# First rows of an attention and dense-layer kernel: where keys, values and M land in the on-chip memory

## The chip, the cores and the metric

The program runs on one core of a Trainium2 chip. A core has TensorE (PE in the profile, with its weight loads as PEld), VectorE (DVE), ScalarE (ACT), GpSimd (POOL) and SyncE (SP), which issues nearly all DMAs here, and 16 DMA engines. The metric is the device time of one execution in microseconds (us), the median of the runs.

## What is computed

For B = 4 batches, H = 8 heads, S = 576 rows and D = 64, causal softmax attention is mixed with a read from a memory M, and the result goes through a dense layer of 512 to 2048 to 512 with a leaky nonlinearity per column:

```python
scores = scale * np.matmul(q, k.transpose(0, 1, 3, 2))      # causal mask, softmax -> a
local = np.matmul(a, v)
mem_out = einsum('bhsd,bhde->bhse', phi(q), M_prev) / (einsum('bhsd,bhd->bhs', phi(q), z_prev)[..., None] + 1e-06)
x = g * mem_out + (1 - g) * local                            # g: sigmoid(beta) by head
h = x @ w_in
out = (np.maximum(h, 0.0) + alpha * np.minimum(h, 0.0)) @ w_out
```

## The kernel before, in words

The 576 rows of a batch are cut into a first block of 64 rows and four blocks of 128. The first 64 rows of all four batches are a case of their own, called Z in the code: two tiles t of two batches each. Their work opens the program; the blocks of the batches follow, and with each group of 256 rows goes its part of the dense layer (moe_in, in the trace matmuls named h; moe_out, named y).

The opening, in order: load_first issues the loads (phases LZ for q, Lz for z_prev, LK for k, LV for v and M). first_scores(t) transposes q and k of tile t on PE (phase tZ; ACT copies the results back), makes the 64 x 64 score products of two batches and eight heads (phase sZ), and DVE reduces each with its mask while ACT takes the exponentials. They land in columns 64 to 127 of each head in the buffer P. prep_vZ (phase v4) finds the largest sums of squares of v and of M over all batches: ACT squares the two value tiles, DVE takes their maximum, PE turns it, DVE reduces it, and scales come of it. prep_phi (phases p40, p41, p4) makes phi(q), its norm, and puts the scaled phi(q) into columns 0 to 63 of P. first_values(t) (phase oZ) scales the probabilities in P, transposes P on PE into a PT buffer, and multiplies that by the tile of 128 partitions that holds M in its lower and v in its upper half, so that one product gives memory part and local part together. Its output is x for the first matmuls of the dense layer in float32 (phases h4_100 to h4_103), which read the first half of w_in (loads LW00 to LW03, conversions C00 to C03 on DVE, from 64-bit floats). 40 matmuls on a tile of ones without any use of their result (phases N and n) stand between the first ones on PE.

In the opening k of Z lies in R[14], the two tiles of M and v in R[15] and R[16]; R holds weights later. q and z lie in buffers with the tag q2. PT is a ring of four buffers of 128 x 1152 words, of which the opening uses two in first_values.

The order is written out by hand: PLACES gives each operation of each phase its place in one list for all engines, and issue sends them out in that list's order. Each engine, and each DMA queue, works through its own in that order. cells and price belong to the tool that found the places: cells tells which parts of a buffer an operation touches, price holds its estimates; they change nothing in the program once PLACES is there.

Of the kernel before, what the change touches and what calls it, by code (L numbers as in the profile page):

```python
# [33 lines left out]
        "38 55"  # L34
    ),
    "LZ1": (
        "39 37"
    ),
    "Lz": (
        "16 17 0"  # L40
    ),
    "LK0": (
        "78 36"
    ),
    "LK1": (
        "75 128"
    ),
    "LV0": (
        "154 79"
    ),  # L50
    "LV1": (
        "194 184"
    ),
    "I": (
        "1 10 2 7 8 9 11"
    ),
    "z": (
        "40 43 56 41 109"
    ),
    "N": (  # L60
        "6 13 14 18 19 20 21 22 23 24 25 27 28 45 46 47"
    ),
    "n": (
        "49 50 51 66 81 82 83 95 96 97 98 101 103 104 105 107 108 115 116 117 118 119 152 153"
    ),
    "J": (
        "30 31 33 42 177 26 32 34 35 48 61 63 67 74 88 90 172 102"
    ),
    "a4": (
        "68 54 87 91"  # L70
    ),
    "K": (
        "5 29"
    ),
    "tZ0": (
        "57 58 59 60 65 110 111 112 113 114 122"
    ),
    "sZ0": (
        "120 121 123 124 125 126 127 129 130 131 132 133 135 136 139 140 146 142 147 143 148 144 141 145 183 182 187 "
        "188 186 202 179 181"  # L80
    ),
    "tZ1": (
        "84 85 86 92 94 134 149 150 151 157 156"
    ),
    "sZ1": (
        "158 159 160 161 162 163 164 165 166 167 168 169 170 171 173 174 204 198 197 214 200 191 208 196 229 199 213 "
        "215 201 233 231 232"
    ),
    "v4": (
        "155 195 205 209 210 216 217 218 460 219"  # L90
    ),
    "p40": (
        "62 64 69 70 175"
    ),
    "p41": (
        "76 77 93 137 138"
    ),
    "p4": (
        "176 178 185 211 220 221 223 180 222 224 251"
    ),  # L100
    "oZ0": (
        "230 235 237 240 241 242 243 244 245 246 247 248 249 262 263 264 265 266 278 279 280 281 282 284 285 295 302 "
        "303 306 307"
    ),
    "oZ1": (
        "234 236 250 252 253 254 255 256 257 258 259 260 261 291 292 293 294 296 297 304 308 309 310 311 312 313 314 "
        "315 316 317"
    ),
    "LW00": (
        "12"  # L110
    ),
    "LW01": (
        "71"
    ),
    "LW02": (
        "80"
    ),
    "LW03": (
        "189"
    ),  # L120
    "LX00": (
        "270"
    ),
    "LX01": (
        "300"
    ),
    "LX02": (
        "238"
    ),
    "LX03": (  # L130
        "276"
    ),
    "C00": (
        "44 52 53"
    ),
    "n0": (
        "203 206"
    ),
    "C01": (
        "72 73 89"  # L140
    ),
    "n1": (
        "207 212"
    ),
    "C02": (
        "99 100 106"
    ),
    "n2": (
        "225 226"
    ),  # L150
    "C03": (
        "190 192 193"
    ),
    "n3": (
        "227 228"
    ),
    "D00": (
        "271 273 283"
    ),
    "c0": (  # L160
        "371 398 399 407 421 459 481 482 623"
    ),
    "D01": (
        "301 345 372"
    ),
    "D02": (
        "269 274 289"
    ),
    "D03": (
        "277 287 290"  # L170
    ),
    "LW10": (
        "401 400"
    ),
    "LW11": (
        "404 444"
    ),
    "C10": (
        "402 403 433"
    ),  # L180
    "c1": (
        "434 449 471 463 478 486 508 557 577 730 646 709"
    ),
    "LW12": (
        "465 466"
    ),
    "C11": (
        "445 447 448"
    ),
    "LW13": (  # L190
        "457 456"
    ),
    "C12": (
        "467 469 470"
    ),
    "C13": (
        "458 461 462"
    ),
    "L0q": (
        "338 239 267"  # L200
    ),
    "L0k": (
        "335 337 336 15"
    ),
    "L0v": (
        "473 474 475 487"
    ),
    "a0": (
        "268 272 275 388"
    ),  # L210
    "bk00": (
        "321 322 323 324 325 318 319 320 326 347"
    ),
    "bk01": (
        "346 351 352 362 348 350 358 370 363 364 366 382 375 376 377 378"
    ),
    "v0": (
        "488 492 493 489 496 497 498 502 503 505 1236 510"
    ),
    "p00": (  # L220
        "305 330 331 385 390"
    ),
    "p01": (
        "349 356 357 387 389"
    ),
    "p0": (
        "425 429 435 468 512 514 515 504 516"
    ),
    "L0Q": (
        "298 286"  # L230
    ),
    "L0K": (
        "405 339"
    ),
    "L0V": (
        "523 522"
    ),
    "A0": (
        "299 288 446 541"
    ),  # L240
    "BK00": (
        "383 384 386 410 411 393 394 395 396 409"
    ),
    "BK01": (
        "438 441 442 443 451 424 427 428 431 432"
    ),
    "V0": (
        "524 537 556 566 591 598 599 684 626 622 629"
    ),
    "r02": (  # L250
        "391 500 501 564 587"
    ),
    "r03": (
        "406 408 495 569 603"
    ),
    "r0": (
        "655 658 682 685 695 698 703 699 708"
    ),
    "h4_100": (
        "327 328 329 332 333 334 340 341 353 354 355"  # L260
    ),
    "s011": (
        "397 476 472 477 485 490 513 517 509 506"
    ),
    "P010": (
        "518 525 526 527 528 531 548 549 550 551 552 559 560"
    ),
    "h4_101": (
        "342 343 344 359 361 365 367 368 374 412 392"
    ),  # L270
    "y4_100": (
        "452 439 453 440"
    ),
    "P011": (
        "519 539 535 543 547 540 570 571 572 574 575 581 582"
    ),
    "s013": (
        "521 532 533 534 554 561 538 555 542 562"
    ),
    "P012": (  # L280
        "565 567 536 568 553 586 590 593 594 595 600 610 611"
    ),
    "o011": (
        "607 608 609 620"
    ),
    "P013": (
        "583 584 613 585 612 601 614 615 616 617 627 628 632"
    ),
    "h4_102": (
        "360 373 379 380 381 415 416 418 419 479 491"  # L290
    ),
    "y4_101": (
        "454 450 455 494"
    ),
    "s015": (
        "563 576 578 588 596 605 580 597 589 606"
    ),
    "P014": (
        "621 624 633 625 592 630 634 635 636 637 661 662 665"
    ),  # L300
    "o013": (
        "666 667 679 680"
    ),
    "P015": (
        "649 657 663 668 631 664 669 670 671 676 677 691 692"
    ),
    "s017": (
        "619 652 650 654 674 672 653 675 651 673"
    ),
    "P016": (  # L310
        "694 696 618 697 573 705 716 717 718 719 720 724 725"
    ),
    "h4_103": (
        "413 414 417 420 422 423 436 437 464 511 507"
    ),
    "y4_102": (
        "480 520 499 558"
    ),
    "o015": (
        "711 713 714 715"  # L320
    ),
    "P017": (
        "683 693 638 712 639 721 726 727 728 729 735 736 740"
    ),
    "s031": (
        "752 753 769 771 772 773 784 783 811 770 796 799"
    ),
    "P030": (
        "812 817 883 816 884 937 820 832 1029"
    ),  # L330
    "o017": (
        "747 748 749 750"
    ),
    "bv00": (
        "797 1032 745 746"
    ),
    "bv01": (
        "765 1031 794 795"
    ),
    "bv02": (  # L340
        "825 1139 733 734"
    ),
    "bv03": (
        "798 808 756 809"
    ),
    "P031": (
        "800 824 801 859 828 866 861 898 969"
    ),
    "h0_100": (
        "688 690 723 759 760 761 762 764 766 775 778"  # L350
    ),
    "y4_103": (
        "529 579 530 602 430 737 739 426 604 704"
    ),
    "h0_101": (
        "689 722 732 763 767 768 780 781 802 804 803"
    ),
    "y0_100": (
        "776 792 847 829"
    ),  # L360
    "h0_102": (
        "779 787 788 789 790 791 793 821 822 833 850"
    ),
    "y0_101": (
        "848 869 849 870"
    ),
    "h0_103": (
        "814 815 818 819 834 835 838 841 842 871 875"
    ),
    "y0_102": (  # L370
        "863 872 864 874"
    ),
    "s033": (
        "856 857 858 946 947 950 997 991 992 862 948 998"
    ),
    "P032": (
        "1087 1092 1097 1093 1131 1151 1094 1103 1241"
    ),
    "y0_103": (
        "880 885 881 886 738 882 1175 656 887 971"  # L380
    ),
    "x4": (
        "369 678"
    ),
    "x0": (
        "751 774"
    ),
    "LW20": (
        "643 640"
    ),  # L390
    "LW21": (
        "645 642"
    ),
    "C20": (
        "644 648 659"
    ),
    "c2": (
        "686 741 757 805 807 810 831 836 1091"
    ),
    "LW22": (  # L400
        "687 660"
    ),
    "C21": (
        "647 700 701"
    ),
    "LW23": (
        "742 702"
    ),
    "C22": (
        "743 744 754"  # L410
    ),
    "LW30": (
        "758 755"
    ),
    "C23": (
        "777 782 785"
    ),
    "S20": (
        "837 845"
    ),  # L420
    "S21": (
        "852 853"
    ),
    "S22": (
        "854 867"
    ),
    "S23": (
        "868 903"
    ),
    "LW31": (  # L430
        "806 786"
    ),
    "C30": (
        "813 830 839"
    ),
    "c3": (
        "843 860 928 1005 1006 1030 1090 1099 1100 1165 1102 1135 1224 1174 1303 1226"
    ),
    "LW32": (
        "846 840"  # L440
    ),
    "C31": (
        "844 851 855"
    ),
    "LW33": (
        "943 944"
    ),
    "C32": (
        "878 902 926 879 901 925"
    ),  # L450
    "C33": (
        "945 966 1000"
    ),
    "S30": (
        "1118 1133"
    ),
    "S31": (
        "1160 1162"
    ),
    "S32": (  # L460
        "1176 1177"
    ),
    "S33": (
        "1220 1222"
    ),
    "S00": (
        "1329 1330"
    ),
    "S01": (
        "1380 1548"  # L470
    ),
    "S02": (
        "1565 1588"
    ),
    "S03": (
        "1591 1673"
# [2343 lines left out]
```

## Time and profile before

| | us |
|---|---|
| median of 3 runs | 548.23 (547.07 to 548.61) |
| profiled execution | 547.6 |
| its span, first to last instruction | 545.8 |
| PE busy | 527.6 (97%) |
| DVE busy | 445.4 (82%) |
| ACT busy | 389.2 (71%) |
| POOL busy | 66.2 (12%) |

The mean granted clock of PE is 0.990. A busy share is an average over the whole span; the rows further down take it apart by stretch of time. Nearly all instructions carry the line of one helper, L1740, so they are told apart by the names of the buffers that they write and read: R is the weights' buffer and also that of k, v and M of the first rows, y, h, s and bank are accumulators, P holds probabilities, PT their transposes.

### The profile page before, as it was taken

The page shows a single profiled execution, that of the slowest core. Times are in us where ns is not written, and L with a number is a line of the kernel's source. Part 1 is how long each engine was busy: PE and PEld are TensorE (multiplying, and loading weights), DVE is VectorE, ACT ScalarE, POOL GpSimd, SP SyncE. Part 2 cuts the span into 40 slices and gives each one's busy share as a digit, 9 for nine tenths or more (in the row PEclk, how much of TensorE's full clock was granted, in tenths as well). Part 3 has the DMA queues.
Part 4 walks back from the last instruction along what each step waited for, and adds up shares of the span by engine and source line. Part 5 has one row for each costly group of instructions (what it writes and reads, how often), then busy time and mean ns, then how long its engine had stood idle before and what let it go on. Part 6 is the DMA issues. An engine that isn't in the chain of part 4 may idle for free. (4 is left out here: it accounts for less than half of the span.)

```text
span 545.8 us, 11936 instructions
## 1 busy us (share of the span) xinstructions
PE 527.6 (97%) x4415; PEld 355.1 (65%) x4415; DVE 445.4 (82%) x1195; ACT 389.2 (71%) x815; POOL 66.2 (12%) x142
## 2 busy tenths in 40 slices
PE   8889999999988999999999999999999999999997
PEld 3578446748556677677756766767686667666863
DVE  3899999999999999999977999998757786662421
ACT  3678899778978689988876988777556767642322
POOL 3000040201011012111111121311102101100000
PEclk8899999999998999999999999999999999999999
DMA  8999915679578979558999765659235556270101
GB/s 166 213 243 364 234 64 182 201 231 223 129 146 181 196 182 218 134 127 166 223 206 185 179 121 99 145 135 190 65 89 119 100 118 142 75 150 11 39 1 38
DMA packets 225650, 82.33 MB, mean 151 GB/s; under 512 B 216100, under 2 KB 216116, under 8 KB 225592
## 3 DMA queue, kind: packets, MB, share of 16 engines
q1 hardware_dynamic: 225408, 81.55, 66.4%
q8 instruction: 34, 0.56, 0.4%
q14 instruction: 24, 0.20, 0.1%
q10 hardware_dynamic: 184, 0.02, 0.0%
HBM read 35.15 MB, written 5.77 MB: 75 GB/s over the span
## 5 line engine op out<-in xcount | busy, mean ns | idle before, releaser
L1740 PE MATMUL y<-R,gg 128*128 128x512 f16 (+1 forms) x832 | 230.6, 396 | 0.4 <-DVE t L1740 0.3
L1740 PE MATMUL h<-x,R 128*128 128x256 f16 x1536 | 212.8, 274 | 1.2 <-DMA x<-xn 1.2
L1740 PEld LDWEIGHTS <-R 128*128 128x128 f16 x1536 | 144.5, 98 | 36.7 <-issue 4.1
L1740 PEld LDWEIGHTS <-gg 128*128 128x128 f16 x768 | 72.7, 98 | 62.4 <-DVE gg L1740 1.0
L1740 POOL TENSOR_SCALAR E<-q,nrm,sm 128x64 f32<-128x64 f32 x112 | 54.7, 501 | 350.4 <-DVE sm L1740 272.9
L1740 ACT ACTIVATE E<-E,mx 128x320 f32<-128x320 f32 (+3 forms) x136 | 80.8, 599 | 22.6 <-DVE mx L1740 20.9
L1740 PE MATMUL bank<-v,PT 128*128 128x64 f16 x1224 | 86.2, 194 | 3.3 <-DVE xn L1740 1.8
L1740 DVE SCALAR_TENSOR_TENSOR P<-E,mx,P 128x640 f16<-128x640 f32 (+3 forms) x112 | 76.2, 699 | 12.2 <-ACT P L1740 11.7
L1740 ACT ACTIVATE P<-E,mx 128x640 f16<-128x640 f32 (+3 forms) x112 | 72.0, 674 | 19.9 <-POOL E L1740 11.4
L1740 PEld LDWEIGHTS <-PT 128*128 128x128 f16 x1224 | 67.1, 98 | 21.8 <-issue 2.7
L1740 DVE SCALAR_TENSOR_TENSOR r<-r,oma,h 128x256 f32<-128x256 f32 x128 | 57.3, 473 | 24.8 <-ACT r L1740 24.5
L1740 DVE CUSTOM_DVE_ANT_0 E<-s,mask,pm 128x576 f32<-128x576 f32 (+3 forms) x96 | 57.8, 613 | 7.6 <-PE s L1740 3.9
L1740 ACT ACTIVATE r<-h 128x512 f32<-128x512 f32 x72 | 42.0, 587 | 27.8 <-PE h L1740 23.5
L1740 ACT ACTIVATE gg<-r,gsc 128x512 f16<-128x512 f32 x56 | 39.5, 714 | 30.6 <-PE y L1740 23.3
L1740 DVE SCALAR_TENSOR_TENSOR gg<-r,gsc,gg 128x512 f16<-128x512 f32 x56 | 41.7, 745 | 20.1 <-ACT gg L1740 18.7
L1740 PE MATMUL s<-k,qT 128*128 128x320 f16 (+5 forms) x136 | 36.6, 290 | 0.2 <-DVE mx L1740 0.2
L1740 PE MATMUL h<-R 128*128 128x256 f32 x144 | 35.6, 391 | 0.0
L1740 PE MATMUL s<-k,qS 128*128 128x192 f16 (+4 forms) x120 | 32.6, 294 | 1.1 <-DMA qS<-qT 1.1
L1740 PEld LDWEIGHTS h<-R 128*128 128x128 f32 x144 | 26.7, 194 | 4.9 <-issue 1.5
L1740 ACT ACTIVATION_READ_ACCUMULATOR E<-E,mx 128x1 f32 x124 | 23.4, 189 | 0.0
L1740 ACT ACTIVATE xn<-bank,xsc 128x256 f16<-128x256 f32 x28 | 13.0, 466 | 10.5 <-PE bank L1740 10.1
L1740 ACT ACTIVATE t<-y,u 128x512 f32<-128x512 f32 x18 | 12.2, 678 | 11.6 <-PE y L1740 9.0
(179 smaller groups left out, 618.8 us busy)
## 6 DMA issues: line engine op xcount, KB each, us to landing
q<-in_q_dram SPq DMA_DIRECT2D x16, 256.0 KB, 4.9
vn<-in_v_dram SPq DMA_DIRECT2D x16, 256.0 KB, 4.4
out_dram<-t SPq DMA_DIRECT2D x16, 256.0 KB, 2.4
kn<-in_moe_w_in_dram SPq DMA_DIRECT2D x6, 512.0 KB, 7.9
kn<-in_moe_w_out_dram SPq DMA_DIRECT2D x6, 512.0 KB, 4.6
kn<-in_k_dram SPq DMA_DIRECT2D x12, 256.0 KB, 4.4
qS<-qT SPq DMA_DIRECT2D x24, 128.0 KB, 2.7
R<-in_moe_w_in_dram SPq DMA_DIRECT2D x4, 512.0 KB, 5.4
```

Of the source, the lines that this page charges most:

```text
L1740: fn(*a, **kw)
```

## The change

In load_first k, v and M of the first rows get three buffers of the ring PT. A transfer takes two batches at once, for q and k as it was for v and M already: q into 64 neighbouring partitions, k into every second partition of 128, v into the odd and M into the even partitions of a tile. A tile's two batches are thereby other ones: tile t now holds batches t and t + 2, and new_group writes their output rows so. The phases LZ0, LZ1, LK0 and LK1 have one DMA each in place of two.

What reads these buffers follows: first_scores takes k at every second column, the score and phi(q) columns of P are interleaved (even columns phi(q), odd columns probabilities), first_values takes v by batch pair and position, prep_vZ reduces even and odd partitions, and z is spread by two copies on ACT in place of one. cells and price learn the new shapes. All places are given anew: 6239 before, 6242 after.

```diff
@@ load_first
-        kz, v0, v1 = (R[i].rearrange("p (t h d) -> p t h d", t=2, h=H) for i in (14, 15, 16))
+        kz, v0, v1 = (wkp.tile([128, 2, H, D], F32, tag="PT", bufs=TB) for _ in range(3))
...
-        for b in range(B):
-            t, ps = b // 2, slice(b % 2 * 64, b % 2 * 64 + 64)
-            work.phase = f"LZ{t}"
-            Y.dma_start(out=qz[ps, t], in_=q[b, :, 0:64, :].rearrange("h p d -> p h d"))
+        for c in range(2):
+            work.phase = f"LZ{c}"
+            Y.dma_start(out=qz[64 * c:64 * c + 64].rearrange("p t h d -> p (t h) d"),
+                        in_=q[2 * c:2 * c + 2, :, 0:64, :].rearrange("b h p d -> p (b h) d"))
...
-        for b in range(B):
-            t, ps = b // 2, slice(b % 2 * 64, b % 2 * 64 + 64)
-            work.phase = f"LK{t}"
-            Y.dma_start(out=nat[Z]["k"][t][ps], in_=k[b, :, 0:64, :].rearrange("h p d -> p h d"))
+        for c in range(2):
+            work.phase = f"LK{c}"
+            Y.dma_start(out=kz[c::2].rearrange("p t h d -> p (t h) d"),
+                        in_=k[2 * c:2 * c + 2, :, 0:64, :].rearrange("b h p d -> p (b h) d"))
...
-            for ps, src in ((slice(64, 128), v[2 * t:2 * t + 2, :, 0:64, :]), (slice(0, 64), M_prev[2 * t:2 * t + 2])):
+            for ps, src in ((slice(1, None, 2), v[2 * t:2 * t + 2, :, 0:64, :]), (slice(0, None, 2), M_prev[2 * t:2 * t + 2])):
@@ prep_vZ
-        V.tensor_reduce(mw, pt.rearrange("p (t c) -> p t c", t=2), axis=AX.X, op=ALU.max)
+        V.tensor_reduce(mw, pt.rearrange("p (c t) -> p t c", t=2), axis=AX.X, op=ALU.max)
@@ prep_phi
-            o = p["P"][i][:, :, 0:D]
+            o = p["P"][i][:, :, 0::2]
@@ first_scores
-            for c in (slice(0, 64), slice(64, 128)):
-                T.matmul(s[c, h, :], lhsT=qT[:, h // 2, c], rhs=kT[:, h % 2, h // 2, c], start=True, stop=True)
+            for c in range(2):
+                cs = slice(64 * c, 64 * c + 64)
+                T.matmul(s[cs, h, :], lhsT=qT[:, h // 2, cs], rhs=kT[:, h % 2, h // 2, c::2], start=True, stop=True)
...
-        E = p["P"][t][:, :, 64:128]
+        E = p["P"][t][:, :, 1::2]
@@ first_values
-        E = P[:, :, 64:128]
+        E = P[:, :, 1::2]
...
-                T.matmul(o[ps, a, c], lhsT=n["v"][t][:, b, h, :], rhs=PT[:, h, c], start=True, stop=True)
+                T.matmul(o[ps, a, c], lhsT=n["v"][b][:, t, h, :], rhs=PT[:, h, c], start=True, stop=True)
@@ new_group
-            [(64 * a, 64 * a + 64, (2 * t + a) * S) for a in range(2)] for t in range(2)]
+            [(64 * a, 64 * a + 64, (t + 2 * a) * S) for a in range(2)] for t in range(2)]
@@ the spread of z
-    A.copy(zs.rearrange("p (b n) -> p b n", b=B), ident[0:B, 0:B][:, :, None].to_broadcast([B, B, 64]))
+    for t in range(2):
+        A.copy(zs[:, 128 * t:128 * t + 128].rearrange("p (b n) -> p b n", b=2),
+               ident[0:B, t:B:2][:, :, None].to_broadcast([B, 2, 64]))
```

The order of SP's loads in the opening, by PLACES, before: LW00, LK0 (second batch), LZ1 (second), LZ0, LZ1, LZ0 (second), LW01, LK1, LK0, M of LV0, LW02, LK1 (second), v of LV0, M of LV1, LW03, v of LV1. After: LW00, LZ1, LZ0, LK0, LW01, LK1, LW02, v and M of LV0, LW03, M and v of LV1. Three small loads (beta, z_prev, alpha) go out on ACT's queue at the very start in both. On PE 15 of the fillers n stand between the transposes of the second tile's k and its scores in the new order (2 in the old one), and on DVE the conversion C00 comes first, and the maximum of batch 0's first q before the scaling of the probabilities.

## Rows read from the trace of the kernel before

**Rows 1.** The page: busy time and share by engine; DVE's tenths in 40 slices.

```profile
PE 527.6 (97%) x4415; PEld 355.1 (65%) x4415; DVE 445.4 (82%) x1195; ACT 389.2 (71%) x815; POOL 66.2 (12%) x142
...
DVE  3899999999999999999977999998757786662421
```

**Rows 2.** Busy time by stretch, columns as headed.

```profile
core 0: us, PE busy (x) PEld busy (x) DVE busy (x) ACT busy (x) POOL busy (x), PEclk, DMA share, GB/s
...
6.79:31.44 24.65, 21.45 (x136) 12.89 (x136) 19.16 (x87) 14.75 (x49) 0.00 (x0) 0.86 1.07 207
36.00:75.00 39.00, 39.00 (x202) 25.42 (x200) 36.98 (x103) 32.47 (x75) 4.16 (x10) 1.00 0.91 259
75.00:140.00 65.00, 63.36 (x400) 42.48 (x399) 63.72 (x153) 55.82 (x115) 8.38 (x16) 1.00 0.64 179
140.00:200.00 60.00, 55.35 (x475) 35.88 (x474) 59.41 (x144) 48.54 (x87) 5.62 (x12) 0.97 0.82 173
200.00:260.00 60.00, 60.00 (x537) 41.65 (x535) 59.11 (x167) 53.07 (x111) 8.52 (x20) 1.00 0.75 164
260.00:540.00 280.00, 277.89 (x2602) 191.49 (x2601) 202.21 (x533) 178.95 (x374) 35.20 (x72) 1.00 0.56 116
```

**Rows 3.** The same table for five short stretches of the opening.

```profile
4.00:6.00 2.00, 1.92 (x5) 0.46 (x3) 0.00 (x0) 0.00 (x0) 1.23 (x2) 1.00 1.27 198
6.00:8.00 2.00, 1.14 (x4) 0.54 (x5) 1.03 (x7) 0.50 (x2) 0.00 (x0) 1.00 0.43 81
16.50:19.50 3.00, 2.98 (x36) 1.87 (x34) 1.44 (x5) 1.16 (x2) 0.00 (x0) 1.00 1.40 148
32.20:33.80 1.60, 1.28 (x10) 1.07 (x11) 1.60 (x3) 0.85 (x2) 0.00 (x0) 1.00 1.29 289
42.00:45.00 3.00, 3.00 (x19) 2.65 (x18) 2.80 (x6) 2.27 (x5) 0.00 (x0) 1.00 1.03 396
```

**Rows 4.** SP's issues (start, duration), and its wait for beta.

```profile
0.73 0.39 SPq L1740 DMA_DIRECT2D R<-in_moe_w_in_dram  x1
...
1.99 5.16 SPq L1740 DMA_DIRECT2D q<-in_q_dram  x4
...
18.63 0.60 SPq L1740 DMA_DIRECT2D R<-in_v_dram  x1
...
SPq L1740 <- DMA gco<-in_beta_dram: 2.6, 1, 2.6
```

**Rows 5.** Timeline: start, duration, engine, operation, count, idle time before, releaser.

```profile
26.75 1.06 ACT L1740 ACTIVATE R<-R 128x1024 f32<-128x1024 f32 x1 [1.18 <-DMA R<-in_v_dram]
...
27.93 0.16 DVE L1740 TENSOR_TENSOR stv<-stv 128x1 f32<-128x1 f32 x1 [0.20 <-ACT R L1740]
...
31.44 1.29 DVE L1740 TENSOR_TENSOR P<-P,zsm 128x512 f32<-128x512 f32 x2
...
32.28 1.07 PE L1740 MATMUL y<-ident,P 128*128 128x128 f32 x8 [1.19 <-DVE P L1740]
...
34.67 2.37 PE L1740 MATMUL s<-PT,R 128*64 128x64 f32 x64
...
37.89 2.34 PE L1740 MATMUL h<-R 128*128 128x256 f32 x10
```

**Rows 6.** Groups of 0 to 36 us: busy us, mean ns, idle before.

```profile
L1740 PE MATMUL h<-ones 128*128 128x512 f16 x40 | 13.7, 484 | 1.0 <-DVE ones L1740 1.0
...
L1740 DVE TENSOR_REDUCE stq<-q 128x1 f32<-128x512 f32 x4 | 2.7, 677 | 0.0
...
L1740 DVE CUSTOM_DVE_ANT_0 P<-s,mz 128x64 f32<-128x64 f32 x16 | 2.7, 218 | 0.0
...
L1740 DVE TENSOR_TENSOR P<-q,nrm 128x512 f32<-128x512 f32 x2 | 1.4, 686 | 0.0
...
L1740 DVE TENSOR_TENSOR P<-P,zsm 128x512 f32<-128x512 f32 x2 | 1.3, 689 | 0.0
...
L1740 DVE TENSOR_SCALAR R<-R 128x512 int32<-128x512 int32 x3 | 1.3, 424 | 0.0
```

More of the change, by code (lines that the diff above doesn't have):

```diff
@@ L33 @@
     "LZ0": (
-        "38 55"
+        "43"
     ),
     "LZ1": (
-        "39 37"
+        "42"
     ),
     "Lz": (
-        "16 17 0"
+        "7 36 0"
     ),
     "LK0": (
-        "78 36"
+        "45"
     ),
     "LK1": (
-        "75 128"
+        "51"
     ),
     "LV0": (
-        "154 79"
+        "60 64"
     ),
     "LV1": (
-        "194 184"
+        "176 175"
     ),
     "I": (
-        "1 10 2 7 8 9 11"
+        "1 23 2 24 25 26 120"
     ),
     "z": (
-        "40 43 56 41 109"
+        "30 29 49 54 31 82"
@@ L120 @@
     ),
     "LX00": (
-        "270"
+        "226"
     ),
     "LX01": (
-        "300"
+        "283"
     ),
     "LX02": (
-        "238"
+        "228"
     ),
     "LX03": (
-        "276"
+        "306"
     ),
     "C00": (
-        "44 52 53"
+        "33 34 35"
     ),
     "n0": (
-        "203 206"
+        "192 209"
     ),
     "C01": (
-        "72 73 89"
+        "74 97 108"
     ),
     "n1": (
-        "207 212"
+        "210 211"
     ),
     "C02": (
-        "99 100 106"
+        "143 155 183"
@@ L399 @@
     ),
     "LW22": (
-        "687 660"
+        "683 653"
     ),
     "C21": (
-        "647 700 701"
+        "626 692 698"
     ),
     "LW23": (
-        "742 702"
+        "741 705"
     ),
     "C22": (
-        "743 744 754"
+        "742 743 744"
     ),
     "LW30": (
-        "758 755"
+        "755 745"
     ),
     "C23": (
-        "777 782 785"
+        "772 786 789"
     ),
     "S20": (
-        "837 845"
+        "822 838"
     ),
     "S21": (
-        "852 853"
+        "839 843"
@@ L1606, in cells @@
         w = 1 if ap.dtype == F16 else 2
+        n = 1
+        for x in ap.tensor.shape[1:]:
+            n *= x
+        n = n * (1 if ap.tensor.dtype == F16 else 2) // w
+        sides = 0, 1
+        if ps == 2 * n:
+            sides = divmod(ap.offset, n)[0] % 2,
+            ps, pn = n, 2 * pn - 1
         p0, o = divmod(ap.offset, ps)
@@ L1616, in cells @@
         m, size = self.known[key], ps * w
-        return sum(m << size * h for h in range(2) if p0 < 64 * (h + 1) and p0 + pn > 64 * h), size
+        return sum(m << size * (2 * h + e) for h in range(2) if p0 < 64 * (h + 1) and p0 + pn > 64 * h for e in sides), size
     def add(self, kind, engine, name, a, kw):
@@ L1692, in price @@
                 return 630, 983, 2186, 343
+            if kb > 200 and (o.tensor.name.startswith("PT") or ins[0].tensor.name.startswith("in_q")):
+                return 640, 1250 if ins[0].tensor.name.startswith("in_q") else 950, 2200, 290
             return (700, 1736, 2490, 290) if kb > 200 else (690, 643, 2157, 150)
```

1008 lines of the change are left out of this document (504 added, 504 removed), and 96 rows, old and new, of tables.

## The prediction

> **What bounds the kernel now.** I read the busy times first, then a table by stretch, then the DMA rates of the first 45 us, then the waits in order of time up to the first dense matmul. TensorE (PE) is busy 97% of the span, VectorE (DVE) 82% [rows 1]; as averages these hide two regimes. In the table by stretch [rows 2] the reader should compare each engine's busy time with the length of its stretch. From 36 to 75 us PE is busy 39.00 of 39 us and DVE 36.98; from 75 to 260 us DVE is busy 182.24 of 185 us (63.72, 59.41 and 59.11) while PE idles 6.29 us in all (1.64 and 4.65, none after 200); from 260 to 540 us PE is busy 277.89 of 280. So from 36 us on the work is packed on PE, on DVE or on both, with 8.4 us of PE idle time in 504 us. In contrast, from 6.79 to 31.44 us DVE is busy only 19.16 of 24.65 us, and much of PE's 21.45 us is no useful work: 40 filler matmuls on a tile of ones take 13.7 us [rows 6]. The slack is in the first 32 us.
>
> What ends last there is a landing. SP issues the last v transfer at 18.63 us [rows 4]; ACT's second square of values starts at 26.75 us, ended by that DMA [rows 5]; from it the chain runs over the DVE maximum (27.93), the scales, DVE's multiplication of the probabilities (31.44) and PE's transposes (32.28, after 1.19 us of idle time for DVE) to the value products (34.67) and the first dense layer (37.89). The DMA engines explain the landing [rows 3]: with only such first-row transfers under way (256-byte runs to 64 neighbouring partitions) they are fully occupied, share 1.40, and move 148 GB/s; with the same runs to 128 partitions, share 1.29, 289 GB/s; with weights, 396 GB/s. And from 6 to 8 us they run dry (share 0.43, 81 GB/s), because the fourth q issue waits 2.6 us on SP for beta [rows 4]; behind it stand all of SP's loads.
>
> **The change, part by part.**
>
> *Landing places.* k, v and M go to every second partition of 128, q stays on 64 neighbouring ones. Bytes up to the last v: four weight halves of 512 KiB, 2.10 MB, and 2.10 MB of q, k, v and M. Before: 2.10/0.396 = 5.3 us and 2.10/0.148 = 14.2 us, together 19.5. The trace took from the first issue at 0.73 to 26.75, 26.0 us, of which I give 2.0 us to the way of the first bytes and 1.2 us to the hole at 6 to 8 us (2 us x (1 - 81/198), by the 198 GB/s of 4 to 6 us [rows 3]); the remaining 22.8 us are 1.17 times the sum, and I keep that factor. After: weights 5.3, q 0.52/0.148 = 3.5, the rest 1.57 MB. No row shows a transfer to every second partition. Its ends are 148 GB/s (no gain, 10.6 us) and 289 GB/s (as with 128 partitions, 5.4 us); a rate below 148 I exclude, since runs and bytes are the same. I take 289: the two rows differ only in the partitions reached, and every second one reaches over all 128. Sum 14.2 us, times 1.17 is 16.6, plus 2.7: the last v at 19.3 us, 7.4 us earlier. At 148 GB/s: 19.5 x 1.17 + 2.7 = 25.5, 1.2 us earlier.
>
> [...]
>
> *Pairs in one transfer.* q and k take 4 issues instead of 8 (v and M had pairs already). SP's issue time is on no path here, but the wait for beta is met at the ninth DMA of the program: before with 1 MiB issued ahead of it, after with 1.75 MiB (a weight, two of q, one of k, a weight), which at the rates above last until about 2.7 + 1.3 + 3.5 + 0.9 + 1.3 = 9.7 us, past the end of the wait at 6.5 us (1.99, three issues of 0.65, then 2.6). The hole closes; its 1.2 us are in the sum.
>
> *Buffers of their own.* kz, v and M move from R[14] to R[16] into three of the four PT buffers. The next writers there are the second first_values transpose (over kz, which has been read long before) and the first units of batch 0, later still; nothing waits, cost 0. first_values(0) now reads both value tiles; it already depended on both through the common maximum, so no wait is new.
>
> *Interleaved operands.* P is written at every second word, and k is read so by the 64 score matmuls. DVE's part is 16 score reductions of 218 ns and two products each of 686 and 689 ns, 6.2 us [rows 6]. The nearest row is the weight conversion that reads every second word: 424 ns for 512 elements, less than the 686 of a dense two-input product, so a stride of two costs a read nothing; no row shows a strided write. Bounds 0 and twice the time (+6.2 us); below 0 nothing, since elements stay the same. I take 0. ACT gets one more small copy for z, at a time when it is busy 0.50 us of 2 [rows 3]; cost 0.
>
> *New order.* All queues are permuted, few operations by much. In front it puts the maximum of batch 0's first q (677 ns [rows 6]) ahead of the product of probabilities and the first weight conversion ahead of beta's arithmetic.
>
> *What is late next.* By the landing alone, PE's transposes would start 5.5 us (32.28 - 26.75) after 19.3, at 24.8 us. But DVE has 19.16 + 0.68 = 19.84 us of work after 6.79, so its last product cannot start before 26.6 us, against 31.44: 4.8 us is the ceiling, and DVE is late next. I leave it 0.8 us of waits, chiefly for the second tile's scores, which stand behind 15 fillers on PE. Gain at the transposes: **4.0 us**. It carries through, because q, k and W_out of the next stage follow on the same queue, earlier too, and from 36 us on DVE and PE are packed. Profiled execution 547.6 (span 545.8 and 1.8 around it) - 4.0 = 543.6; the median of the runs is 0.6 above that execution, so 548.2 - 4.0 = **544.2 us**.
>
> **Rivals.**
> 1. *The landing gets no faster*: every second partition at 148 GB/s. The last v lands 1.2 us earlier: 547.0. For it: the row is missing. Against: the factor of 1.95 between rows with equal runs. Chance 0.12.
> 2. *The gain reaches the transposes and is given back between 75 and 260 us*, where the order is new and DVE is full: PE idle time there grows from 6.3 to some 9.5 us. 547.5. For it: a wait that a new order moves costs directly there; against: the amount of DVE work is unchanged. Chance 0.13.
> 3. *Slower*: in the same stretch the new order starves PE (of transposed probabilities, or of values behind DVE) for more than 4.0 + 1.6 = 5.6 us beyond the 6.3 of before, so that idle time nearly doubles; at 6.5 us more, 550.7. The clock is part of that price: idle PE time goes with granted clock 0.97 in 140 to 200 us. For it: 4.65 us of idle time sit there already. Against: DVE is full there in any order. (Strided DVE writes at twice the time, +6.2 us, would come out near 550 too; I count them here.) Chance 0.08.
> 4. *More*: the front gains its whole 4.8 us and the new order also removes half of the 4.65 us at 140 to 200 us: 541.1. Chance 0.12.
>
> **How the numbers follow.** Forecast, a gain of 2.5 to 4.8 us, 543.4 to 545.7: 0.55. A change of 0.3% (1.6 us) is about what a measurement of this kernel can tell from none. Faster by more: the forecast, rival 4 and half of rival 1 (where the landing is better than its bound): 0.55 + 0.12 + 0.06 = 0.73. Same: half of rival 1 and rival 2: 0.19. Slower: 0.08. The range 541.2 to 548.0 leaves out rival 3, half of rival 4 and the upper part of rival 2, under 0.2.
>
> **What would show it.** After the change, ACT's second square should start at 19 to 21 us; a stretch with only v and M on the queue should move well over 200 GB/s; the DMA share at 6 to 8 us should be near 1; DVE's idle time between its first work and the product of probabilities should fall from 5.5 to about 1 us; PE's transposes of P should start near 28.3 us and the first dense run near 34. The table by stretch, moved by 4 us, should show the same PE idle time (8.4 us) as before. The prediction is wrong if the landing comes early and PE's transposes do not (then DVE, ACT or a filler holds them), or if they come early and the idle time after 36 us grows.

## The result: 0.84% faster, and the profile after

| us | before | after |
|---|---|---|
| median | 548.93 (547.07 to 551.05) | 544.38 (542.94 to 545.80) |
| profiled execution | 547.6 | 544.01 |
| its span | 545.8 | 542.2 |
| mean granted clock of PE | 0.990 | 0.999 |

The ratio of the times is 0.9916, with a 95% interval of 0.9888 to 0.9944: a gain of 4.5 us, and in the profiled execution of 3.6 us (that of the kernel before, with 547.6 us, lies 1.3 us under its median). The forecast was 544.2 us. The granted clock is higher after the change, but it does not make the gain: of the runs with a mean granted clock of 0.997 or more, the 15 of the changed kernel (here, in e0 and in e10) have a median of 544.9 us and the 6 of the kernel before one of 549.7. The list of places holds 6242 operations before the change and 6239 after it: four DMAs fewer, one copy more.

The page of the changed kernel, busy times and DVE's tenths in 40 slices (for [rows 1]); the line of the helper is now L1750:

```profile
PE 523.0 (96%) x4415; PEld 352.9 (65%) x4415; DVE 444.0 (82%) x1195; ACT 391.4 (72%) x816; POOL 67.8 (13%) x142
...
DVE  4999898999999999999988899988777876752222
```

The second digit of DVE, the slice from 13.6 to 27.1 us, is now a 9, that is 90% or more. The table by stretch (for [rows 2]) has the columns us, PE, PEld, DVE, ACT and POOL busy (instructions), granted clock, DMA share, GB/s:

```profile
6.79:31.44 24.65, 22.44 (x207) 14.61 (x208) 23.45 (x97) 17.84 (x55) 0.00 (x0) 1.00 1.07 266
36.00:75.00 39.00, 38.39 (x181) 23.66 (x180) 36.32 (x111) 33.52 (x81) 7.87 (x16) 1.00 0.74 229
75.00:140.00 65.00, 63.52 (x389) 41.10 (x389) 63.26 (x143) 54.62 (x106) 6.95 (x9) 1.00 0.69 187
140.00:200.00 60.00, 52.23 (x474) 35.34 (x475) 58.93 (x145) 49.13 (x87) 6.18 (x12) 1.00 0.84 177
200.00:260.00 60.00, 59.93 (x548) 41.52 (x546) 58.37 (x162) 52.03 (x110) 9.22 (x20) 1.00 0.76 164
260.00:540.00 280.00, 276.16 (x2581) 190.65 (x2578) 198.66 (x528) 177.93 (x371) 33.29 (x72) 1.00 0.57 114
```

In the opening (first line) DVE idles 1.20 us in place of 5.49, and the DMA engines move 266 GB/s in place of 207. In the fourth line PE idles 7.77 us in place of 4.65. The timeline of the opening (for [rows 5]; start, duration, engine, operation, count, idle time before and what ended it):

```profile
20.37 1.06 ACT L1750 ACTIVATE R<-PT 128x1024 f32<-128x1024 f32 x1
21.60 0.22 DVE L1750 CUSTOM_DVE_ANT_0 P<-s,mz 128x64 f32<-128x64 f32 x1 [0.29 <-PE s L1750]
...
22.03 0.16 DVE L1750 TENSOR_TENSOR stv<-stv 128x1 f32<-128x1 f32 x1
...
25.95 0.69 DVE L1750 TENSOR_TENSOR P<-P,zsm 128x512 f32<-128x512 f32 x1
...
26.79 1.07 PE L1750 MATMUL y<-ident,P 128*128 128x128 f32 x8 [0.15 <-DVE xsc L1750]
27.43 0.69 DVE L1750 TENSOR_TENSOR P<-P,zsm 128x512 f32<-128x512 f32 x1
...
32.62 0.70 PE L1750 MATMUL h<-R 128*128 128x256 f32 x2
```

ACT's second square of values starts at 20.37 (before: 26.75), PE's transposes of P at 26.79 (before: 32.28), the first dense run at 32.62 (before: 37.89). The opening is 5.5 us shorter at the transposes and 5.3 at the dense run; 3.6 us of it are left at the end of the span. In this execution the second square does not wait for a DMA, for ACT is busy until it starts; the last v, issued at 14.64, had landed by then.

### The profile page after: what moved, and what is told of

The parts are those of the page before. It is cut to its first block, busy times and chain, and to the rows that moved or that the text cites. A ratio compares the mean times of both kernels' runs of the same rounds, so it can differ in the third digit from the quotient of the medians.

```text
span 542.2 us, 11944 instructions
## 1 busy us (share of the span) xinstructions
PE 523.0 (96%) x4415; PEld 352.9 (65%) x4415; DVE 444.0 (82%) x1195; ACT 391.4 (72%) x816; POOL 67.8 (13%) x142
## 4 chain that ended last, share of the span: by engine, by line
PE 72%; DVE 17%; DMA 5%; ACT 3%; issue 2%; DVEq 0%; SPq 0%
PE h L1750 30%; PE y L1750 29%; PE s L1750 7%; PE bank L1750 5%; DVE R L1750 5%; DVE P L1750 3%; DVE E L1750 2%; DMA PT<-P 2%; DVE gg L1750 2%; DVE r L1750 1%; DVE q L1750 1%; DMA q<-in_moe_w_in_dram 1%; DMA k<-k 1%; ACT PT L1750 1%; DMA t<-part 1%
## 5 line engine op out<-in xcount | busy, mean ns | idle before, releaser
L1750 PE MATMUL y<-R,gg 128*128 128x512 f16 (+1 forms) x832 | 236.5, 396 | 1.0 <-DVE t L1750 0.9
L1750 PE MATMUL h<-x,R 128*128 128x256 f16 x1536 | 216.6, 273 | 1.8 <-DVE r L1750 1.7
L1750 PEld LDWEIGHTS <-R 128*128 128x128 f16 x1536 | 144.1, 98 | 40.2 <-issue 2.2
L1750 PEld LDWEIGHTS <-gg 128*128 128x128 f16 x768 | 72.8, 98 | 58.5 <-issue 1.8
L1750 POOL TENSOR_SCALAR E<-q,nrm,sm 128x64 f32<-128x64 f32 x112 | 54.6, 499 | 330.7 <-DVE sm L1750 255.5
L1750 ACT ACTIVATE E<-E,mx 128x320 f32<-128x320 f32 (+3 forms) x136 | 80.8, 600 | 19.0 <-DVE mx L1750 17.9
L1750 DVE SCALAR_TENSOR_TENSOR P<-E,mx,P 128x512 f16<-128x512 f32 (+3 forms) x112 | 76.2, 699 | 13.7 <-ACT P L1750 12.6
L1750 PE MATMUL bank<-v,PT 128*128 128x64 f16 x1224 | 79.7, 193 | 3.3 <-DMA PT<-P 2.1
L1750 ACT ACTIVATE P<-E,mx 128x640 f16<-128x640 f32 (+3 forms) x112 | 72.3, 674 | 13.5 <-POOL E L1750 7.8
L1750 PEld LDWEIGHTS <-PT 128*128 128x128 f16 x1224 | 63.3, 98 | 21.2 <-DMA PT<-P 2.7
L1750 ACT ACTIVATE r<-h 128x512 f32<-128x512 f32 x72 | 42.1, 588 | 45.4 <-PE h L1750 40.0
L1750 DVE SCALAR_TENSOR_TENSOR r<-r,oma,h 128x256 f32<-128x256 f32 x128 | 57.2, 474 | 21.2 <-ACT r L1750 21.0
L1750 DVE SCALAR_TENSOR_TENSOR gg<-r,gsc,gg 128x512 f16<-128x512 f32 x56 | 41.7, 746 | 24.6 <-ACT gg L1750 23.9
L1750 DVE CUSTOM_DVE_ANT_0 E<-s,mask,pm 128x192 f32<-128x192 f32 (+3 forms) x96 | 57.0, 611 | 4.4 <-PE s L1750 2.8
L1750 ACT ACTIVATE gg<-r,gsc 128x512 f16<-128x512 f32 x56 | 39.9, 713 | 23.3 <-PE y L1750 18.9
L1750 PE MATMUL s<-k,qT 128*128 128x448 f16 (+5 forms) x136 | 36.5, 290 | 1.2 <-DMA k<-k 1.2
L1750 PE MATMUL h<-R 128*128 128x256 f32 x144 | 35.3, 384 | 0.7 <-DVE gg L1750 0.7
L1750 PE MATMUL s<-k,qS 128*128 128x192 f16 (+4 forms) x120 | 33.2, 294 | 2.2 <-DMA qS<-qT 2.2
L1750 PEld LDWEIGHTS h<-R 128*128 128x128 f32 x144 | 26.0, 191 | 6.0 <-issue 2.2
L1750 ACT ACTIVATION_READ_ACCUMULATOR E<-E,mx 128x1 f32 x124 | 23.3, 188 | 0.0
L1750 ACT ACTIVATE R<-R,wsc 128x1024 f16<-128x1024 f32 x16 | 18.3, 1143 | 6.3 <-DVE R L1750 3.9
L1750 DVE SCALAR_TENSOR_TENSOR R<-R,wsc 128x1024 f16<-128x1024 f32 x16 | 20.5, 1281 | 0.0
```

The source lines that it names most:

```text
L1750: fn(*a, **kw)
```

## The experiments

Each time is the median of one kernel, beside the median of the kernel before on the same chip; the ratio stands with its 95% interval. "Second square" is ACT's square of the second value tile, "transposes" PE's first transposes of P, as in the timeline above.

### e1: all of the change but the landing places

```diff
-    Y.dma_start(out=kz[c::2].rearrange("p t h d -> p (t h) d"),
+    Y.dma_start(out=kz[64 * c:64 * c + 64].rearrange("p t h d -> p (t h) d"),
...
-    for ps, src in ((slice(1, None, 2), v[...]), (slice(0, None, 2), M_prev[...])):
+    for ps, src in ((slice(64, 128), v[...]), (slice(0, 64), M_prev[...])):
...
-        E = p["P"][t][:, :, 1::2]
+        E = p["P"][t][:, :, 64:128]
```

The pairs, the buffers of their own and the new order stay.

> The changed kernel with k, v and M landing on 64 neighbouring partitions again (columns of P and reads of k follow); pairs, PT buffers and the new order stay. Theory 'the landing places make the gain': the last first-row v lands some 5 us later than in the changed kernel (ACT's second square at 25 to 26.5 us instead of 20.4), PE's transposes of P start near 31 us instead of 26.8, and the time goes back by 3 to 5 us, to 547.5 to 549. Rival 'pairs and order make the gain': second square at 20 to 21.5 us, transposes near 27, time 544 to 545.

Measured: 549.35 us beside 549.6, ratio 0.9998 (0.9980 to 1.0016). Two stretches of this kernel in which values are under way together with the next q, by the table of windows, and then the like stretch of the changed kernel:

```profile
20.00:22.00 2.00, 0.86 (x4) 0.20 (x2) 1.06 (x3) 2.00 (x8) 0.00 (x0) 1.00 1.41 180
21.00:23.00 2.00, 0.94 (x7) 0.51 (x7) 1.94 (x7) 1.96 (x9) 0.00 (x0) 1.00 1.31 170
```

```profile
18.00:20.00 2.00, 2.00 (x11) 0.85 (x9) 2.00 (x12) 1.96 (x9) 0.00 (x0) 1.00 1.21 246
```

The DMA engines are fully occupied in both (share 1.2 to 1.4), with 246 GB/s where k, v and M go to every second partition and 170 to 180 where they go to neighbours; the next q is part of both figures. The time from issue to landing tells the same, as the profile lists it by buffer (KB each, median us), for v in the changed kernel and then in e1:

```profile
PT<-in_v_dram SPq DMA_DIRECT2D x2, 256.0 KB, 5.6
```

```profile
PT<-in_v_dram SPq DMA_DIRECT2D x2, 256.0 KB, 8.3
```

M takes 6.1 us in the one and 9.2 in the other. In the three profiles that land on neighbours (the kernel before, e1, e6) v and M take 8.0 to 9.2 us, and in the eleven that land on every second partition 4.0 to 7.2. The second square starts at 24.81 here, ended by the last v, and the transposes at 30.75, which is 1.5 us earlier than in the kernel before, without any gain in the time. Without the landing places nothing of the gain is left. Pairs, buffers and order bring nothing by themselves that the time shows; the interval leaves room for some 1 us.

### e2 and e5: the landing places alone, in R and in buffers of their own

e2 is the kernel before, in its order and with one batch in each transfer, but with the new landing places and what reads them:

```diff
-    Y.dma_start(out=nat[Z]["k"][t][ps], in_=k[b, :, 0:64, :].rearrange("h p d -> p h d"))
+    Y.dma_start(out=nat[Z]["k"][t][b % 2::2], in_=k[b, :, 0:64, :].rearrange("h p d -> p h d"))
...
-    for ps, src in ((slice(64, 128), v[...]), (slice(0, 64), M_prev[...])):
+    for ps, src in ((slice(1, None, 2), v[...]), (slice(0, None, 2), M_prev[...])):
```

> The kernel before with k, v and M on every second partition, and nothing else: one batch per transfer of q and k, buffers in R, old order. Theory 'landing places': the stretch of first-row transfers moves over 220 GB/s in place of 148, the second square starts at 21 to 23 us (the hole at 6 to 8 us stays), transposes of P near 28 to 30 us in place of 32.3, time 545 to 547. Rival 'order needed': the second square is early, but DVE's old order keeps the transposes at 31 to 32 us, and the time stays at 548 to 549.

Measured: 552.23 us beside 549.6, ratio 1.0059 (1.0039 to 1.0079). It is slower, and no theory had that. SP's waits in the first 40 us of e2 (waiting queue, released by: us in total, times, longest):

```profile
SPq L1740 <- DVE scr L1740: 6.8, 1, 6.8
SPq L1740 <- DVE str L1740: 3.3, 1, 3.3
SPq L1740 <- ACT P L1740: 2.0, 1, 2.0
SPq L1740 <- DMA gco<-in_beta_dram: 1.8, 1, 1.8
```

and its timeline:

```profile
6.47 0.62 SPq L1740 DMA_DIRECT2D R<-in_moe_w_in_dram  x1
...
13.78 1.31 SPq L1740 DMA_DIRECT2D R<-in_k_dram  x2
...
18.96 0.69 DVE L1740 SCALAR_TENSOR_TENSOR R<-R 128x512 int32<-128x512 int32 x1 [4.96 <-DMA R<-in_M_prev_dram]
```

SP stands still for 6.8 us, from 7.09 to 13.78, before it issues k, and DVE's conversion of a weight in R stands 4.96 us for the landing of M. Neither has anything to do with the other's data: k and M lie in other parts of R, which is one tile cut into 17 slices. From 6.79 to 31.44 us the DMA engines are busy to 0.66 only, at 177 GB/s, and the transposes start at 35.13, later than before. It is not the landing that is late: once issued, v takes 4.1 us and M 4.0 to land, in the kernel before 8.0 and 8.1. In the kernel before, where the same buffers take the same data on 64 neighbouring partitions, SP has the wait for beta of [rows 4], one of 1.6 us for ACT and one of 0.7 in that stretch, and nothing like these. That the waits are set as if a transfer to every second partition touched all of R is inferred from them; e5 tests it, with one line beside e2:

```diff
-        kz, v0, v1 = (R[i].rearrange("p (t h d) -> p t h d", t=2, h=H) for i in (14, 15, 16))
+        kz, v0, v1 = (wkp.tile([128, 2, H, D], F32, tag="PT", bufs=TB) for _ in range(3))
```

> The kernel before with the landing places of the change and its three PT buffers, but one batch per transfer of q and k and the old order. Theory 'landing places make the gain, and need buffers of their own, because in R each strided transfer is made to wait for the weights' conversions and the conversions for it': SP's stop of 6.8 us at 7 us, seen with the strided landing in R, is gone, the last square starts at 23 to 24.5 us, transposes of P at 29 to 30.5 us in place of 32.3, time 545.5 to 547. Rival 'without pairs it does not work': SP still stops, transposes at 32 us or later, 548.5 or more.

Measured: 544.43 us beside 548.84, ratio 0.9914 (0.9883 to 0.9944). SP's waits in the same stretch of e5:

```profile
SPq L1740 <- ACT P L1740: 3.1, 1, 3.1
SPq L1740 <- DMA gco<-in_beta_dram: 1.8, 1, 1.8
SPq L1740 <- DVE R L1740: 0.8, 1, 0.8
```

The stop of 6.8 us is gone, and the time is that of the whole change, without pairs and in the old order; it is 1 us less than the theory had. The wait for beta is still there, 1.8 us, and so is the hole in the DMA (share 0.59 from 6 to 8 us, 130 GB/s); they cost nothing that the time shows. Nor does the front alone tell the end: the transposes start at 29.53, 2.75 us earlier than before, and the span of that execution is 541.8 us, 4.0 shorter; in e1 1.5 us at the transposes bring nothing. That the landing places make the gain is shown by taking them away (e1) and by putting them in alone (e5); how many of the front's microseconds reach the end is not explained run by run.

### e6: the buffers alone

The line of e5 in the kernel before, and nothing else.

> The kernel before with k, v and M of the first rows in three PT buffers, on 64 neighbouring partitions, nothing else. Theory 'buffers cost and bring nothing by themselves': as the kernel before, ratio 0.997 to 1.003, transposes at 32 to 32.5 us. Rival 'the buffers alone free SP or the conversions': last square and transposes at least 1 us earlier, ratio under 0.997.

Measured: 548.78 us beside 548.84, ratio 0.9995 (0.9973 to 1.0017). By themselves the buffers are worth nothing that the time shows. In the profile the transposes start at 33.81, later than either theory had: v landed late (second square at 28.02), and eight products of PE ahead of them took 3.66 us (from 30 to 34 us the granted clock is 0.57). e2 and e5 show that they are nonetheless what the landing places need here.

### e3 and e4: the old order

e3 is the changed kernel with the places of before (for the phases LZ and LK, which have one DMA each now, the first of their places). e4 has the new order up to about 83 us and the old one behind it.

```diff
-PLACES = the new places
+PLACES = the places of before
```

> The changed kernel (landing places, pairs, buffers) in the order of the kernel before. Theory 'landing and pairs': hole at 6 to 8 us partly closed, second square at 20 to 22 us, transposes at 28 to 29 us, time 544.5 to 546.5, so that the new order is worth 1 to 2 us at most. Rival 'the new order is half of it': transposes at 30 us or later, time 547 or more.

> The changed kernel with its own order for the first 700 places (some 83 us) and the order of the kernel before for all that follows. Theory 'the new order gives back 1 to 2 us after 100 us': the shift of 5.2 us at 80 us is kept, PE idle time of the 60 us around 136 to 196 us is back near 4.7 us, time 542.5 to 543.7. Rival 'the loss has nothing to do with the order' (DVE is full there, or the transfers of that stretch meet the earlier ones): time 544 to 545, as in the changed kernel.

Measured: e3 545.99 us, ratio 0.9928 (0.9901 to 0.9956); e4 543.75, ratio 0.9900 (0.9880 to 0.9919), both beside 549.6. In the old order the second square starts at 23.89 and the transposes at 29.52, in e4 at 21.12 and 27.05. e3's square and transposes are later than its first theory had and earlier than its rival's. Between e3 and e4 the new order gains 2.5 us in the opening, between e3 and the three executions of the changed kernel 1.3 to 2.7; but at the end this can't be told, since the intervals of e3, e4, e5 and the changed kernel (0.9888 to 0.9944) overlap. In e4 PE idles 5.59 us from 140 to 200 us, in the changed kernel 7.77. e4 again, under the label e11 and beside the changed kernel again (e10, below):

> The kernel with the new order for 700 places and the old one behind, beside the changed kernel on the same chip. Theory 'the new order gives back 1 to 2 us after 100 us': at least 0.8 us below the changed kernel. Rival: within 0.5 us of it.

Measured: e11 544.83 us, ratio 0.9922 (0.9891 to 0.9953); e10 545.77, ratio 0.9943 (0.9923 to 0.9962), both beside 548.8. PE's idle time from 140 to 200 us again falls, from 7.62 to 5.52 us, and the time again by 0.9 us, but inside the intervals. That the idle time is the order's is shown: from 75 to 260 us PE idles 8.7 to 9.3 us in four profiles that differ from e4 and its like only in the order behind 83 us (changed, e0, e10, e8) and 6.0 to 7.5 us in e4, e9 and e11. Whether it costs time at the end stays open. From the transposes to the end of the span, the profiled executions in the new order took 514.7 to 517.6 us (six, three of them of the changed kernel, middle 515.6), and those in the old order, at least behind 83 us, 512.3 to 517.0 (eight, middle 514.6): a difference of 1 us with a scatter of 3 to 5.

### e7: less work on DVE

Two of the products phi(q) * z (0.67 us each on DVE) go to POOL.

```diff
-PZ = [1, 1, 1, 1, 1]
+PZ = [1, 1, 1, 1, 0]
```

> The changed kernel with the two products of phi(q) and z of the first rows on POOL in place of DVE (PZ of the first rows 0); same values. Theory 'DVE is late next in the opening': with 1.2 us of work less on DVE before the products of P, PE's transposes come at 25.6 to 26.2 us in place of 26.8 and the time falls by 0.6 to 1.2 us against the changed kernel of this series. Rival 'DVE only waits elsewhere for that time' (for the second scores behind PE's fillers, or for POOL, whose products are slower): transposes at 26.7 us or later, same time as the changed kernel or more.

Measured: 545.51 us beside 548.84, ratio 0.9940 (0.9916 to 0.9964), no better than the changed kernel. From the timeline of e7:

```profile
11.78 1.27 POOL L1750 TENSOR_TENSOR t<-q,q 128x512 f32<-128x512 f32 x1 [6.94 <-DVE q L1750]
14.79 1.67 POOL L1750 TENSOR_TENSOR t<-q,q 128x512 f32<-128x512 f32 x1 [1.74 <-DVE q L1750]
```

```profile
12.25 1.08 DVE L1750 TENSOR_SCALAR R<-R 128x512 int32<-128x512 int32 x1 [0.37 <-DMA R<-in_moe_w_in_dram]
...
16.49 0.69 DVE L1750 TENSOR_REDUCE nrm<-t 128x8 f32<-128x512 f32 x1 [0.58 <-POOL t L1750]
```

Of the 1.3 us that DVE gives away, a conversion that runs beside POOL's product takes back 0.65 (1.08 for 0.43), and the wait for the second product 0.58. The test is therefore weak: DVE hardly got any time, and the first tile's score reductions start at 17.10 (changed kernel: 17.02). The values landed late in this execution (second square at 22.37), and the 14 products ahead of the transposes took PE 4.97 us in place of 3.29, so that these started at 29.67:

```profile
24.86 4.97 PE L1750 MATMUL h<-R 128*128 128x256 f32 x14
```

PE's granted clock from 24.86 to 29.83 is 0.66 there. By DVE, whose last step before them ends at 28.30, they could have started 1.4 us earlier. The two products stand ahead of the second tile's scores; the work of DVE that stands behind them, of which more below, the edit leaves as it was. So e7 does not tell whether less work on DVE would bring the transposes forward.

### e8 and e9: the values ahead of the last weight

In e8, the changed kernel, LW03 goes out behind the loads of LV1; its conversion C03 on DVE and the products n3 on PE that read it move back with it, behind the first tile's scaling and value products. e9 is the same edit in e4.

```diff
-SP: ... LW03, M of LV1, v of LV1
+SP: ... M of LV1, v of LV1, LW03
```

> The changed kernel with the last two loads of v and M put ahead of the fourth weight half (LW03), and that half's conversion on DVE (C03, 1.8 us) and its two clock products on PE behind the products and transposes of P. Theory 'after the change the landing of the last v still decides, with DVE close behind': the last square starts 1.0 to 1.5 us earlier than in the changed kernel of this series, PE's transposes of P 1.0 to 2.0 us earlier, and the first dense products as much, if the late conversion stays under the transposes; time 0.8 to 1.8 us below the changed kernel. Rival 'DVE alone is late, by other work than C03', or 'the conversion is late next': transposes earlier but the first dense products at the same time, time within 0.5 us of the changed kernel.

> The same edit on the kernel with the new order for 700 places and the old one behind. If both gains add up: 542 to 543 us, the fastest of all; if the new order gives nothing back in truth, as the one before this in the list.

> The changed kernel, as the mark for this series: 543.5 to 545.5 us; the last square of values at 20.4 to 22.4 us, as its two profiles showed.

Measured, all beside 548.8: e8 544.71 us, ratio 0.9929 (0.9909 to 0.9948); e9 544.14, ratio 0.9915 (0.9892 to 0.9938); the changed kernel 545.77 (e10). None is told apart from another. The timelines of e10 and then of e8 tell why:

```profile
21.44 1.06 ACT L1750 ACTIVATE R<-PT 128x1024 f32<-128x1024 f32 x1 [1.44 <-DMA PT<-in_v_dram]
...
21.64 0.23 DVE L1750 CUSTOM_DVE_ANT_0 P<-s,mz 128x64 f32<-128x64 f32 x1 [0.72 <-PE s L1750]
...
27.38 1.06 PE L1750 MATMUL y<-ident,P 128*128 128x128 f32 x8 [0.15 <-DVE xsc L1750]
```

```profile
20.44 1.04 ACT L1751 ACTIVATE R<-PT 128x1024 f32<-128x1024 f32 x1
...
21.77 0.22 DVE L1751 CUSTOM_DVE_ANT_0 P<-s,mz 128x64 f32<-128x64 f32 x1 [1.15 <-PE s L1751]
...
26.94 1.06 PE L1751 MATMUL y<-ident,P 128*128 128x128 f32 x8 [1.14 <-DVE xsc L1751]
```

The second square starts 1.0 us earlier (as early as in the first profile of the changed kernel), and the transposes start only 0.44 us earlier: DVE now waits 1.15 us for PE's scores of the second tile, which are no earlier than before. The dense run starts even later (33.66 in e8, 33.21 in e10), for the moved conversion is late next.

### e0: the changed kernel again

> The changed kernel itself once more, as the mark for the others of this series: 543.5 to 545.5 us, transposes of P at 26.8 us, the last square of values at 20.4 us.

Measured: 544.79 us beside 548.84, ratio 0.9926 (0.9895 to 0.9956). In this execution v landed late: the square starts at 22.32 and the transposes at 28.25, both later than expected.

### What holds the transposes

All profiles in the new order of the opening, set side by side (us; the first three columns are starts, the next two the distances to the transposes; e7, with other work on DVE and POOL, stands apart):

| | second square | first reduction of the second tile's scores | transposes | from the square | from the reduction |
|---|---|---|---|---|---|
| changed | 20.37 | 21.60 | 26.79 | 6.42 | **5.19** |
| e8 | 20.44 | 21.77 | 26.94 | 6.50 | **5.17** |
| e9 | 20.36 | 21.70 | 26.74 | 6.38 | **5.04** |
| e11 | 21.76 | 23.86 | 29.05 | 7.29 | **5.19** |
| e4 | 21.12 | 21.45 | 27.05 | **5.93** | 5.60 |
| e10 | 21.44 | 21.64 | 27.38 | **5.94** | 5.74 |
| e0 | 22.32 | 21.98 | 28.25 | **5.93** | 6.27 |
| e1 | 24.81 | 24.05 | 30.75 | **5.94** | 6.70 |

The transposes start 5.93 us after the second square or 5.0 to 5.2 us after the first reduction of the second tile's scores, whichever is later (bold). So two chains meet there: the landing of the values, and the second tile's scores. In the three executions of the changed kernel they end 0.5 to 1.1 us apart, and now one, now the other is last. Both run into the same queue of DVE. From the maximum that follows the square to the transposes it is busy 4.69 of 4.76 us in the changed kernel (4.69 of 4.76 in e10, 4.68 of 4.75 in e0); columns as in the table by stretch:

```profile
22.03:26.79 4.76, 4.03 (x19) 2.98 (x18) 4.69 (x30) 3.81 (x22) 0.00 (x0) 1.00 1.08 306
```

The distances in bold are thus nearly all DVE's work behind the last wait, some of it (reductions of the second tile's scores, a step of a weight's conversion, the maximum of batch 0's q) by its data not needed for the first transposes. No run took that work away. A third chain is close: PE's 14 products end 0.15 us before the transposes, except in e8 and e9, and in e7 they are the last. The row of e11 is one in which PE ran at a granted clock of 0.51 from 10 to 16 us (the changed kernel: 1.00), and all of its opening came late.

## Why the prediction was right, and where its steps were not

- **What bounds the kernel: right.** The slack was in the first 32 us, behind the last landing. e1, with the landing as late as 24.81, gains nothing; e5, with nothing but the landing places in buffers of their own, gains as much as the whole change.
- **Landing places: right that the rate goes by the partitions reached, a little too much in its size.** Every second partition was taken at 289 GB/s, which gave 19.3 us; the stretch that comes nearest has 246, with the next q in it. With that rate in the same sum, 1.57 MB take 6.4 us, and the last v lands at 20.5 us. The second square starts at 20.37, 21.44 and 22.32 in three executions of the changed kernel, in the latter two ended by v and outside the 19 to 21 us that the prediction named. The other bound, 148 GB/s, gave 25.5; e1, at 170 to 180, has 24.81. So rival 1 is out: e1 comes near the sum at 148 GB/s, and the changed kernel near that at 246. The length of the runs doesn't decide here, for e1 and the changed kernel move the same runs of 256 bytes, at 170 to 180 and at 246 GB/s. Why the partitions reached set the rate no run shows. Nor does one show the 2.0 us that the sum gave to the way of the first bytes: before and after the change the DMA share is 0.00 up to 1.70 us and 1.02 and 1.33 from 1.70 to 1.80, so the first bytes move 1.0 us after the first issue at 0.73. With 1.0 us in its place the factor is 1.22 in place of 1.17, and the same sum puts the last v at 19.1 us in place of 19.3.
- **Pairs and the hole at 6 to 8 us: closed, and worth nothing that the time shows.** The window from 6 to 8 us has a DMA share of 0.97 in place of 0.43. The sum had 1.2 us for it; e5 has the hole still and the same time, within intervals of some 1.6 us to either side. The reason given was not right: the wait for beta is gone from SP, but SP is held up all the same, not behind 1.75 MiB but at its fourth issue, behind 1 MiB as before. That issue takes 3.34 us, the next one of k 0.61:

```profile
2.68 3.34 SPq L1750 DMA_DIRECT2D PT<-in_k_dram  x1
...
7.15 0.61 SPq L1750 DMA_DIRECT2D PT<-in_k_dram  x1
```

The DMA share is 1.05 in these 3.34 us, so the engines do not run dry; what holds the issue the profile doesn't name.
- **Buffers of their own, cost 0: right as a cost, and it missed what they do.** Taking them for a mere move left out that the landing places alone, in R, make the kernel slower (e2, 0.6% over the kernel before, where e5 is 0.9% under it). The prediction asked what waits on the new buffers, and not what would wait on the old ones with the new shape.
- **Interleaved operands, cost 0: right.** In the groups of the opening the 16 score reductions and the two kinds of products take what they took in [rows 6], though they now write every second word (and the 64 score products that read k so take 225 ns each, at a granted clock of 1.00 in that stretch; before 271, at 0.86):

```profile
L1750 DVE CUSTOM_DVE_ANT_0 P<-s,mz 128x64 f32<-128x64 f32 x16 | 2.7, 211 | 0.3 <-PE s L1750 0.3
...
L1750 DVE TENSOR_TENSOR P<-P,zsm 128x512 f32<-128x512 f32 x2 | 1.4, 686 | 0.0
...
L1750 DVE TENSOR_TENSOR P<-q,nrm 128x512 f32<-128x512 f32 x2 | 1.3, 651 | 0.0
```

- **What is late next: half right.** DVE's idle time fell to 1.20 us, as told, and the gain at the transposes was 5.5, 4.0 and 4.9 us in three executions (predicted: 4.0). But the ceiling of 4.8 us was passed. It put all of DVE's work of before ahead of the last product; the new order has the first tile's product at 25.95 and the second tile's, with what it needs, behind it at 27.43, and PE starts after the first. That DVE is late next holds in this form: it works without a gap from the last wait to the transposes, and what ends that wait is one of the two chains of the table above. The second tile's scores, which the prediction gave "0.8 us of waits", are one of them, and e8 ends on it; the landing is the other, which the prediction no longer had in the way.
- **"It carries through": wrong in its reason.** Moved by 4 us, the table should have shown the same 8.4 us of PE idle time from 36 us on; it is 12.1 us (11.4 and 11.5 in e0 and e10). By the prediction's own sign, transposes that come early and idle time that grows, this step failed. From 75 to 260 us PE idles 9.32 us in place of 6.29, in 140 to 200 us by waits like these, from the timeline of PE of the changed kernel:

```profile
160.38 1.92 PE L1750 MATMUL h<-x,R 128*128 128x256 f16 x16 [1.73 <-DVE r L1750]
...
167.35 0.32 PE L1750 MATMUL s<-k,qS 128*128 128x192 f16 x2 [2.21 <-DMA qS<-qT]
```

That is the mechanism of rival 2, which had some 9.5 us; e0 and e10 have 9.1 and 8.7. Its time of 547.5 did not come, for two reasons: the opening gained 5.5 us in place of 4.0, and the granted clock in 140 to 200 us is 1.00 in place of 0.97, at most 1.8 us for those 60 (an estimate, as if PE were the limit all the time; in e10 it is 0.97). In the profiled executions the predicted gain of 4.0 us came near by luck: a front gain that was too small and a loss that was left out nearly cancel (5.5 - 1.9 = 3.6). The size of that loss hangs on one execution of the kernel before that was faster than its median; between the medians the gain is 4.5 us, with 4.0 to 5.5 at the transposes. So the idle time behind the front is the new order's (e4, e9, e11), and what it costs stays open. Luck is also part of how close the forecast time is: the kernel before measured 548.9 us here, 0.7 above the 548.2 that the sum started from, and the gain was 0.5 larger.
- **Rivals 3 and 4.** PE was not starved beyond the front's gain (3.0 us more idle time from 75 to 260 us, not over 5.6), and the 4.65 us at 140 to 200 us grew in place of shrinking.

No version here beats the changed kernel by more than the measurement can tell.

## What to carry to other kernels

Where a chain ends in a landing, look at how many bytes the DMA engines move while they are full: with the same runs, landing on every second partition of 128 went with 246 GB/s where 64 neighbouring ones had 170 to 180. Before such a transfer goes into a slice of a buffer that others use too, look at what its issue and the buffer's other users wait for: in a buffer of its own it gained 0.9%, in the shared one it lost 0.6%. And a slack of several microseconds is closed only up to the next chain: list the chains that meet at the engine that waits, with their distances, and the work that stands in the queue behind the last of these waits, before pricing what is late next.

## What the runs showed of the hardware

- A wait of PE of about 2 us is sometimes followed by a lower granted clock, and sometimes not. In e3 the wait of 2.02 us for x ends at 294.51, and the window from 290 to 300 us has the clock at 0.83:

```profile
290.00:300.00 10.00, 7.98 (x52) 5.67 (x51) 6.45 (x18) 4.46 (x10) 0.00 (x0) 0.83 1.02 207
```

In the changed kernel the wait of 2.21 us at 167.35 leaves it at 1.00; in e10, where the same wait is 2.99 us, the window from 160 to 170 us has 0.88. In e3's six runs, 543.5 to 548.3 us, the three shorter ones have a mean granted clock of 0.997 and the three longer ones 0.987 to 0.992; in the six of the changed kernel there is no such order. What decides whether the clock falls no run shows.
- A conversion step of DVE with one input took 1.08 us in place of 0.43 beside a product on POOL (e7, once; the product ended at 13.05 us, the step at 13.33); a reduction of DVE beside the second product took its usual 0.67. What makes the one longer and not the other the trace doesn't show.
